# One area for normed tiles and three form pairs, a later load for the third chunk, and one more projection turned by DMA

## The chip, the cores and the metric

The kernel runs on one core of a Trainium2 chip. The metric is the device time of one execution in microseconds (us). The core's engines work in parallel, each through its own list of instructions in order: PE (TensorE, the matrix multiplier, with PEld for its weight loads), DVE (VectorE), ACT (ScalarE), POOL (GpSimd) and SP (SyncE, which here only issues transfers). Transfers are moved by 16 DMA engines; results of PE lie in PSUM until DVE or ACT fetches them.

## The reference

Two layers follow each other on 2048 rows of 576 numbers. Each layer adds a windowed attention (32 heads of 18 numbers, a window of 8 keys at distances 0, 2, ... 14) and a feed-forward block (FFN, 576 to 4608 to 576 with SiLU) to its input; both take the layer-normed input. Weights are the same in both layers.

```python
x = A_x
x = x + _A_ref(_layernorm(x, axis=-1), A_wqkv, A_wo)
x = x + _B_ref(_layernorm(x, axis=-1), B_w1, B_w2)
x = x + _A_ref(_layernorm(x, axis=-1), A_wqkv, A_wo)
x = x + _B_ref(_layernorm(x, axis=-1), B_w1, B_w2)

# in _A_ref: off = jnp.arange(W) * dil, W, dil = 8, 2
logits = jnp.einsum("bhsd,bhswd->bhsw", q, kg) * scale
o = jnp.einsum("bhsw,bhswd->bhsd", softmax(logits), vg)
# _B_ref: silu(x @ w1) @ w2
```

## The kernel before

The 2048 rows are cut into four chunks of 512 rows (`NC = 4`), each of four tiles of 128 rows (`NJ = 4`). Two layers of four chunks make eight stages, s = 0 to 7. A stage is: the products for queries, keys and values (L672), the attention on DVE (L770 to L811), the projection with the output weights `wo` (`project`, L842), and the FFN.

Every product is made of f16 parts: a number is split into a high part (`hi`, on ACT) and the rest (`lo`, on DVE), and the large products of the two are summed. Stages 0 and 1 use a plain FFN (`ffn`: L1181 for the first matrix, L1183 to L1188 for SiLU and the split of its result `h`, L1200 for the second). From stage 2 on (`S2 = 2`) `ffn_pairs` takes the 36 blocks of the hidden layer in 18 pairs q, with seven products P1 to P7 of 256 rows by sums and differences of halves in place of eight (L1084), which DVE adds together (L1091) out of four PSUM tiles (z0, z1, misc0, misc1) that the next products need; then SiLU, the split of h (L1114 on ACT, L1117 on DVE) and L1139 for the second matrix, in six groups of three pairs. The sums and differences of the weights, `wfs`, are made once, by `prepare(q)` on POOL, DVE (L989, L1004) and ACT (L997) during stages 1 and 2, stored, and loaded by `load_wf` (L1014), seven loads for each q, in every stage from 2 on.

What the products take on the other side is made by `forms` (L1021): the four tiles of a chunk are normed, sums and differences are formed, and for each of the seven P a pair of two "yf" tiles is filled by ACT (L1049, L1050) and DVE (L1054, L1055) and turned by two DMA transposes on SP (L1059) into an "xf" tile in the area xb or its neighbours. There are two places for such a pair: one shares its memory with the tiles "yh" (area YH; a normed tile, or one of the attention's output, that is to be turned), the other with "y" and the turned tiles "oT" of the projection (area YO). A place can be filled again once its two transposes have landed. A third place for the pair's hidden sums, "ha", also lies in YO; it is used in stage 2 only. In the profile the names yh and yo stand for everything in these two areas.

`transposed` turns a 128 by 1152 tile in one of two ways: on PE, nine transposes into PSUM (L456) and one copy by ACT (L458), or by one DMA transpose on SP (L460). `project` takes the first for s < 2 and the second from s = 2 on.

The order of the work is not written out. Each operation is given to `Plan` with an engine, a cost, a priority and what it reads and writes; the plan simulates the engines with these costs, takes at each moment the operation of the best priority that has its inputs and its places, and writes the lists of the engines in the order that comes out. Tiles of most names are handed out by turns, and SP has at most eight transfers on the way. So any edit that changes a place, a wait or a cost can change the lists of all engines from there on.

Of the kernel before, what the change touches and what calls it, by code (L numbers as in the profile page):

```python
# [16 lines left out]
P = 128  # L17
# [246 lines left out]
def sliding_attention_silu_ffn(ctx: ExitStack, tc: tile.TileContext, x, wqkv, wo, w1, w2, out):  # L264
# [48 lines left out]
    WQA, W1A, HA = area("wq", 2 * 30 * UC * 2), area("w1", 12 * KB * 2), area("h", 10 * 2 * TB * 2)  # L313
    HSA, YO = area("hs", 3 * TB * 4), area("yo", 2 * 9 * P * 2)

# [22 lines left out]
    tag("mx", 2, [P, NJ, UH], F32, turns=False)  # L338
    part("y", YO, 2, [D], F32, turns=False)
    part("oT", YO, 2, [9, P], F16, turns=False)  # L340
    YH = area("yh", 2 * 9 * P * 2)
    part("yh", YH, 2, [9, P], F16, turns=False)
    parts("yf", [(YH, 0), (YO, 0)], [2, KB], F16)
    tag("wo", 1, [P, 10, D], F16)
# [9 lines left out]
    part("hs", HSA, 3, [TB], F32)  # L354
    parts("ha", [(HSA, 0), (XB, 14 * KB * 2), (YO, 0)], [4, 2 * P], F32)
    parts("hq", [(HSA, 0), (WQA, 20 * 3 * UC), (WQA, 20 * 3 * UC + 32 * P)], [4, 2 * P], F32)
# [109 lines left out]
    gate = []  # L466
    formed = []
    begun = []
    highs = []
# [348 lines left out]
    def project(s, o, xs):  # L818

        pr_ = s - 1.0  # L820
        for j in range(NJ):
            oh, oT, acc = Buf("yh"), Buf("oT"), Buf("acc")

            def hi(j=j, oh=oh):
                f, src = fl(T(oh)), T(o)[:, j, :]
                if s < 2:
                    nc.scalar.activation(f[:, 0:D], src, AF.Copy, scale=SO)
                else:
                    nc.vector.tensor_scalar(f[:, 0:D], src, SO, None, op0=ALU.mult)

            def lo(j=j, oh=oh):
                halves_lo(T(o)[:, j, :], fl(T(oh)), SO)
            src = [(o, j, u) for u in range(NU)] + ["so"]
            op(*(("ACT", 0.7) if s < 2 else ("DVE", 0.45)), hi, src, [(oh, 0)], pr_)
            op("DVE", 0.86, lo, src + [(oh, 0)], [(oh, 1)], pr_)
            transposed(oh, lambda oT=oT: T(oT), oT, j, pr_, s < 2)

            def mm(oT=oT, acc=acc):
                pl = list(passes(lambda k: T(oT)[:, k, :], lambda k: T(WO)[:, k, :]))
                for n, (a, b) in enumerate(pl):  # L840
                    for h in range(2):
                        nc.tensor.matmul(T(acc)[:, h, 0:288], a, b[:, h * 288:(h + 1) * 288],  # L842
                                         start=n == 0, stop=n == len(pl) - 1)
            op("PE", 3.43, mm, [(oT, j)] + [(WO, k) for k in range(10)], [acc], pr_)
            op("DVE", 0.75, lambda j=j, acc=acc: add_to(xs[j], acc, DO), [acc, "so"], [xs[j]], pr_ - 0.3)
# [165 lines left out]

    def load_wf(q, i, prio):
        w = Buf("wf")
        op("SP", 0.38, lambda: nc.sync.dma_start(fl(T(w)), wfs[q][:, i * KB:(i + 1) * KB]), [("wfs", q, i // 4)], [w], prio, nbytes=P * KB * 2)  # L1014
        return w
# [5 lines left out]
    def forms(xs, prio, home="yb", late=[]):  # L1021
# [21 lines left out]
        for n in P_ORDER:  # L1043
            r = Y_ROW[n]
            f, x = Buf("yf"), Buf("xf")
            for a in range(2):
# [5 lines left out]
                def lo(f=f, a=a, r=r):  # L1052
# [5 lines left out]
                done = op("DVE", 0.48, lo, [(ys[a], r), (f, a, 0)], [(f, a, 1)], prio)  # L1058
                op("SP", 1.26, lambda f=f, a=a, x=x: nc.sync.dma_start_transpose(T(x)[:, :, a * P:(a + 1) * P], T(f)[:, a]),  # L1059
                   [(f, a, 0), (f, a, 1)], [(x, a)], prio, nbytes=P * KB * 4)  # L1060
            out[n] = x
# [3 lines left out]
    def ffn_pairs(s, xf, xs):  # L1065
# [3 lines left out]
        for g, n in enumerate(G2):  # L1069
            hb, wbs = [], []  # L1070
            for q in range(q0, q0 + n):
                wf = {k: load_wf(q, W_ROW[k], pd) for k in P_ORDER}
                w2b = [load_w2(2 * q + f, pd, after=begun[-2:-1] if q > q0 + 1 else ()) for f in range(2)]
# [239 lines left out]
```

## Time and profile before

| | us |
|---|---|
| median of 3 runs (2149.39 to 2159.14) | 2149.91 |
| the profiled execution | 2152.02 |
| its span | 2149.9 |
| PE busy | 2110.2 (98%) |
| DVE busy | 1639.7 (76%) |
| ACT busy | 976.4 (45%) |
| POOL busy | 364.5 (17%) |

The span is the profiled part of one execution, 2.1 us less than that execution's own time. "Idle before" is the time for which an engine had nothing running ahead of an instruction, and the name behind the arrow is what ended that. Times within the trace are from the start of the span. PEclk is the clock that PE was granted, as a share of the full one. Lines are those of the kernel before.

### The profile page before, as it was taken

Reading aid. Unit: us, or ns where it says so; the run is one execution under the profiler, and the core shown is the slowest. Engines: PE = TensorE matmul, PEld = TensorE weight load, DVE = VectorE, ACT = ScalarE, POOL = GpSimd, SP = SyncE. Lnnn points to the kernel's source line nnn. Section 1 sums busy time; section 2 is a strip of 40 time slices with the busy share of each in tenths; the row PEclk is TensorE's granted clock in tenths of the full one; section 3 lists DMA queues with packets and bytes.
Section 4 is the critical chain, followed back from the end, with each engine's and each line's share of the span. In section 5 each row is a group of like instructions: output and inputs, shape, how many; then the busy total and the mean of one; then the engine's idle time right before and its main releaser. Section 6 shows DMA issues by size and latency. Waiting matters only on the chain.

```text
span 2149.9 us, 41260 instructions
## 1 busy us (share of the span) xinstructions
PE 2110.2 (98%) x16198; PEld 1578.7 (73%) x16198; DVE 1639.7 (76%) x2585; ACT 976.4 (45%) x1803; POOL 364.5 (17%) x585
## 2 busy tenths in 40 slices
PE   6999999999999999999999999999999999999999
PEld 3556566656666888876788777887788877888887
DVE  8999999999987997648975499755997669853322
ACT  7555787654443553344433343243443434333332
POOL 2224656332432240001100010000000000000000
PEclk9999999999999999999999999999999999999999
DMA  6587778597879987775757756586555965666551
GB/s 181 152 229 250 240 250 266 169 305 256 243 167 258 307 247 215 164 211 171 211 139 191 220 168 179 131 237 190 175 166 142 254 185 158 166 152 197 157 168 62
DMA packets 334233, 426.18 MB, mean 198 GB/s; under 512 B 145608, under 2 KB 262708, under 8 KB 330072
## 3 DMA queue, kind: packets, MB, share of 16 engines
q1 hardware_dynamic: 293720, 293.19, 49.1%
q0 software_dynamic: 38304, 129.28, 18.8%
q8 instruction: 126, 2.06, 0.4%
q10 hardware_dynamic: 2016, 1.11, 0.2%
q14 instruction: 67, 0.55, 0.1%
HBM read 307.32 MB, written 67.68 MB: 174 GB/s over the span
## 4 chain that ended last, share of the span: by engine, by line
PE 71%; DMA 5%; DVE 3%; ACT 1%; issue 0%; SPq 0%; POOL 0%; DVEq 0%; ACTq 0%
PE acc L1139 28%; PE misc L1084 12%; PE z L1084 12%; PE acc L1200 5%; PE z L672 4%; PE acc L842 4%; PE misc L672 3%; PE z L1181 3%; DMA yo<-yh 1%; DMA w<-wfs 1%; DMA xb<-yh 1%; DMA kvs<-kvs 1%; DVE prs L803 0%; DVE prs L770 0%; DVE prs L810 0%
## 5 line engine op out<-in xcount | busy, mean ns | idle before, releaser
L1139 PE MATMUL acc<-w,h 128*128 128x288 f16 x5184 | 669.0, 286 | 0.6 <-DVE x L1148 0.6
L1139 PEld LDWEIGHTS <-h 128*128 128x128 f16 x5184 | 507.7, 98 | 125.7 <-issue 0.8
L1084 PEld LDWEIGHTS <-w 128*128 128x128 f16 x5292 | 517.8, 98 | 73.8 <-issue 5.3
L1084 PE MATMUL misc<-xb,w 128*128 128x256 f16 x2660 | 339.2, 273 | 2.4 <-DVE yo L1091 1.8
L1084 PE MATMUL z<-xb,w 128*128 128x256 f16 x2632 | 332.6, 273 | 3.7 <-DVE hs L1091 2.3
L849 DVE SCALAR_TENSOR_TENSOR x<-acc,d,x 128x576 f32<-128x576 f32 x183 | 148.5, 813 | 140.4 <-PE acc L1139 137.6
L1200 PE MATMUL acc<-w,h 128*128 128x288 f16 x1728 | 217.0, 287 | 3.9 <-DMA w<-wfs 3.7
L672 PEld LDWEIGHTS <-xa 128*128 128x128 f16 x1344 | 131.8, 98 | 111.3 <-issue 2.9
L1200 PEld LDWEIGHTS <-h 128*128 128x128 f16 x1728 | 169.6, 99 | 49.4 <-ACT h L1185 4.0
L770 DVE TENSOR_TENSOR prs<-qt,kvs 128x2304 f32<-128x2304 f32 x64 | 163.5, 2554 | 13.3 <-DMA kvs<-kvs 12.3
L803 DVE TENSOR_TENSOR prs<-kvs,pe 128x1152 f32<-128x1152 f32 x128 | 170.2, 1351 | 0.6
L774 DVE TENSOR_REDUCE lg<-prs 128x128 f32<-128x2304 f32 x64 | 163.1, 2548 | 1.1
L810 DVE TENSOR_TENSOR prs<-prs 128x1152 f32<-128x1152 f32 (+1 forms) x128 | 135.1, 1055 | 2.9
L1181 PE MATMUL z<-xb,w 128*128 128x512 f16 x588 | 130.6, 382 | 3.3 <-ACT w L919 2.6
L1117 DVE SCALAR_TENSOR_TENSOR h<-wq,sh,h 128x1024 f16<-128x1024 f32 x60 | 76.9, 1281 | 71.2 <-ACT h L1114 71.1
L672 PE MATMUL z<-wq,xa 128*128 128x432 f16 x658 | 124.7, 346 | 0.0
L842 PE MATMUL acc<-wo,yo 128*128 128x288 f16 x896 | 114.2, 286 | 3.3 <-DMA yo<-yh 1.5
L1088 ACT ACTIVATE wq<-z 128x256 f32<-128x256 f32 x94 | 35.5, 380 | 172.3 <-PE z L1084 172.3
L1181 PEld LDWEIGHTS <-w 128*128 128x128 f16 x588 | 57.6, 98 | 73.3 <-ACT w L919 3.1
L842 PEld LDWEIGHTS <-yo 128*128 128x128 f16 x896 | 87.4, 98 | 27.8 <-DMA yo<-yh 2.5
L751 POOL DMA_DIRECT2D kvs<-kvs x64 | 33.8, 535 | 415.0 <-ACT qt L741 415.0
L672 PE MATMUL misc<-wq,xa 128*128 128x432 f16 x518 | 100.9, 350 | 0.8 <-ACT qt L741 0.8
(226 smaller groups left out, 2566.6 us busy)
## 6 DMA issues: line engine op xcount, KB each, us to landing
w<-wfs SPq DMA_DIRECT2D x756, 160.0 KB, 3.5
w<-w2s SPq DMA_DIRECT2D x252, 288.0 KB, 4.3
wq<-wqs SPq DMA_DIRECT2D x17, 1080.0 KB, 6.2
kvs<-kd POOLq DMA_DIRECT2D x8, 1584.0 KB, 8.5
w<-w1s SPq DMA_DIRECT2D x36, 320.0 KB, 5.4
wfs<-xa POOLq DMA_DIRECT2D x18, 640.0 KB, 4.6
w2s<-w POOLq DMA_DIRECT2D x36, 288.0 KB, 4.2
w1s<-wq POOLq DMA_DIRECT2D x30, 320.0 KB, 4.1
```

The source lines that it names most:

```text
L672: nc.tensor.matmul(T(m)[:, :3 * UC], a, b, start=n == 0, stop=n == len(pl) - 1)
L770: nc.vector.tensor_tensor(T(pr), T(qt)[:, j:j + 2, None, :].to_broadcast([P, 2, W, UC]), win(T(kv), j, 2), op=ALU.mult)
L774: nc.vector.tensor_reduce(T(lg)[:, j:j + 2].rearrange("p a w h -> p (a w h)"), T(pr).rearrange("p a w (h d) -> p (a w h) d", d=DH), axis=A ...
L803: nc.vector.tensor_tensor(T(pr)[:, a].rearrange("p w (h d) -> p w h d", d=DH), v, T(pe)[:, j + a, :, :, None].to_broadcast([P, W, UH, DH]) ...
L810: nc.vector.tensor_tensor(t[:, :, 0:h, :], t[:, :, 0:h, :], t[:, :, h:2 * h, :], op=ALU.add)
L842: nc.tensor.matmul(T(acc)[:, h, 0:288], a, b[:, h * 288:(h + 1) * 288], start=n == 0, stop=n == len(pl) - 1)
L849: nc.vector.scalar_tensor_tensor(t, T(acc)[:, :, 0:288], d, t, op0=ALU.mult, op1=ALU.add)
L1084: nc.tensor.matmul(t, w[:, u, :], v[:, r, :], start=first and m == 0, stop=m == 6, skip_group_check=True)
L1117: op("DVE", 1.2, lambda hq=hq, h=h, sc=sc: nc.vector.scalar_tensor_tensor(T(h)[:, 1].rearrange("p f t -> p (f t)"), T(hq).rearrange("p r t ...
L1139: nc.tensor.matmul(T(acc)[:, h, 0:288], T(hb[t])[:, a, f, j * P:(j + 1) * P], T(wbs[t][f])[:, w, h * 288:(h + 1) * 288], start=t == 0 and ...
L1181: nc.tensor.matmul(T(z), v, u, start=m == 0, stop=m == len(pl) - 1)
L1200: nc.tensor.matmul(T(acc)[:, h, 0:288], T(hb[q])[:, a, j * P:(j + 1) * P], T(wbs[q][0])[:, w, h * 288:(h + 1) * 288], start=q == 0 and m = ...
```

## The change

Three edits. First, the areas YH and YO become one area, YY, of the same total size (9216 bytes per partition). The tiles yh lie in its first half, y and oT in its second half (from 4608), and three places for form pairs lie at 0, 2560 and 5120; the third place of ha moves to 5120. So three form pairs can be under way at once, and the first two no longer fit the border between yh and oT: the second pair overlaps both. Second, in stage 2 the seven loads of `wfs` for pair q = 1 wait for the last two of the 14 form transposes of that stage. Third, `project` uses the DMA transpose from s = 1 on, where it was from s = 2 on.

```diff
-    HSA, YO = area("hs", 3 * TB * 4), area("yo", 2 * 9 * P * 2)
+    HSA, YY = area("hs", 3 * TB * 4), area("yy", 4 * 9 * P * 2)
+    YO = 2 * 9 * P * 2
...
-    part("y", YO, 2, [D], F32, turns=False)
-    part("oT", YO, 2, [9, P], F16, turns=False)
-    YH = area("yh", 2 * 9 * P * 2)
-    part("yh", YH, 2, [9, P], F16, turns=False)
-    parts("yf", [(YH, 0), (YO, 0)], [2, KB], F16)
+    part("y", YY, 2, [D], F32, at=YO, turns=False)
+    part("oT", YY, 2, [9, P], F16, at=YO, turns=False)
+    part("yh", YY, 2, [9, P], F16, turns=False)
+    part("yf", YY, 3, [2, KB], F16)
...
-    parts("ha", [(HSA, 0), (XB, 14 * KB * 2), (YO, 0)], [4, 2 * P], F32)
+    parts("ha", [(HSA, 0), (XB, 14 * KB * 2), (YY, YO + 512)], [4, 2 * P], F32)
...
-            transposed(oh, lambda oT=oT: T(oT), oT, j, pr_, s < 2)
+            transposed(oh, lambda oT=oT: T(oT), oT, j, pr_, s < 1)
...
-    def load_wf(q, i, prio):
+    def load_wf(q, i, prio, after=()):
...
-        op("SP", 0.38, lambda: nc.sync.dma_start(fl(T(w)), wfs[q][:, i * KB:(i + 1) * KB]), [("wfs", q, i // 4)], [w], prio, nbytes=P * KB * 2)
+        op("SP", 0.38, lambda: nc.sync.dma_start(fl(T(w)), wfs[q][:, i * KB:(i + 1) * KB]), [("wfs", q, i // 4)], [w], prio, nbytes=P * KB * 2, after=after)
...
-                op("SP", 1.26, lambda f=f, a=a, x=x: nc.sync.dma_start_transpose(T(x)[:, :, a * P:(a + 1) * P], T(f)[:, a]),
-                   [(f, a, 0), (f, a, 1)], [(x, a)], prio, nbytes=P * KB * 4)
+                turnings.append(op("SP", 1.26, lambda f=f, a=a, x=x: nc.sync.dma_start_transpose(T(x)[:, :, a * P:(a + 1) * P], T(f)[:, a]),
+                   [(f, a, 0), (f, a, 1)], [(x, a)], prio, nbytes=P * KB * 4))
...
-                wf = {k: load_wf(q, W_ROW[k], pd) for k in P_ORDER}
+                wf = {k: load_wf(q, W_ROW[k], pd, turnings[-2:] if s == S2 and q == 1 else ()) for k in P_ORDER}
```

In the changed kernel the line numbers are one higher from L314 on (L1059 becomes L1060, and so on), and yh and yo are both called yy. The lists are the same up to the projection of stage 1, at some 385 us of the profiled execution of before; they differ on all engines from there to about 950 us, and are nearly the same again behind it, but for the third form pair, which comes earlier. PE loses 36 transposes and their 36 weight loads, ACT the four copies of L458 and three table loads; SP has four DMA transposes more.

In the projection of stage 1 the order of PE is now: four groups of 18 L1201, 14 L1182, 56 L843 (tiles 0 and 1 of the projection), 14 L1182, 18 L1201, 28 L843 (tile 2), 18 L1201, 28 L843 (tile 3). The transposes of tiles 0 and 1 stand on SP ahead of the two loads of w1s2 and w1s3, that of tile 2 behind them, and that of tile 3 behind w1s4 and w1s5; the last two wait for PE, which has to be done with tiles 0 and 1, since oT has two places.

The first place shown is SP towards the end of the first FFN matrix of stage 1, where the forms of stage 2 are turned (about 649 to 671 us of before). w1_70<-wfs0 and wfs1 are the loads for q = 0 and q = 1, xb_67 is where the xf tiles lie. Before:

```order
L1014 DMA w1_70<-wfs0_196 128x640 [waits DMAHW4_49,PE_49]
L1059 DMA_TRANSPOSE xb_67<-yh_91 128x5x128 [waits DMAHW5_49,DVE_49,Activation_49]
L1014 DMA w1_70<-wfs0_196 128x640 [waits DMAHW6_49,PE_49]
L1014 DMA w1_70<-wfs0_196 128x640 [waits DMAHW7_49,PE_49]
L1014 DMA w1_70<-wfs0_196 128x640 [waits DMAHW0_49,PE_49]
L1014 DMA w1_70<-wfs0_196 128x640 [waits DMAHW1_49,PE_49]
L1014 DMA w1_70<-wfs1_197 128x640 [waits DMAHW2_49,DMASW7_49,PE_49]
L1014 DMA w1_70<-wfs1_197 128x640 [waits DMAHW3_49,DMASW6_49,PE_49]
L1014 DMA w1_70<-wfs1_197 128x640 [waits DMAHW4_49,PE_49]
L1059 DMA_TRANSPOSE xb_67<-yo_73 128x5x128 [waits DVE_49,DMAHW5_49,PE_49,Activation_49]
```

The same place in the changed kernel:

```order
L1015 DMA w1_70<-wfs0_195 128x640 [waits DMAHW4_49,PE_49]
L1015 DMA w1_70<-wfs0_195 128x640 [waits DMAHW5_49,PE_49]
L1060 DMA_TRANSPOSE xb_67<-yy_73 128x5x128 [waits DVE_49,DMAHW6_49,PE_49,Activation_49]
L1060 DMA_TRANSPOSE xb_67<-yy_73 128x5x128 [waits DMAHW7_49,DVE_49,Activation_49]
L1060 DMA_TRANSPOSE xb_67<-yy_73 128x5x128 [waits DVE_49,DMAHW0_49,PE_49,Activation_49]
L1060 DMA_TRANSPOSE xb_67<-yy_73 128x5x128 [waits DMAHW1_49,DVE_49,Activation_49]
L1060 DMA_TRANSPOSE xb_67<-yy_73 128x5x128 [waits DVE_49,DMAHW2_49,PE_49,Activation_49]
L1060 DMA_TRANSPOSE xb_67<-yy_73 128x5x128 [waits DMAHW3_49,DVE_49,Activation_49]
L1015 DMA w1_70<-wfs1_196 128x640 [waits DMAHW4_49,DMASW7_49]
L1015 DMA w1_70<-wfs1_196 128x640 [waits DMAHW5_49,DMASW6_49]
```

The last six transposes now stand in one row between the loads for q = 0 and those for q = 1; before, three loads of q = 1 stood ahead of them. Earlier on SP the first six transposes now follow each other at once (before, three, then six loads of w2s between), and the fourth pair's two follow with loads of w2s and w1s between them.

The second place is DVE in the projection of stage 2 (about 564 to 573 us of before), behind the addition of an FFN result to tile x_81. L829 and the two L443 are the split of a tile of the attention's output, which SP then turns, L1188 is the split of h, L1004 is part of `prepare`. Before:

```order
L849 SCALAR_TENSOR_TENSOR x_81<-acc_104,d_269,x_81 128x576 [waits PE_49]
L1004 SCALAR_TENSOR_TENSOR xa<-wq,accw,xa 128x4x256 [waits Activation_49]
L1004 SCALAR_TENSOR_TENSOR xa<-wq,accw,xa 128x4x128 [waits Activation_49]
L1004 SCALAR_TENSOR_TENSOR xa<-wq,accw,xa 128x3x256 [waits Activation_49]
L1004 SCALAR_TENSOR_TENSOR xa<-wq,accw,xa 128x3x128 [waits Activation_49]
L1188 SCALAR_TENSOR_TENSOR h<-hs,sh_266,h 128x512 [waits Activation_49]
L829 TENSOR_SCALAR yh<-o,so 128x576 [waits DMAHW2_49]
```

The same place in the changed kernel:

```order
L850 SCALAR_TENSOR_TENSOR x_81<-acc_103,d_268,x_81 128x576 [waits PE_49]
L830 TENSOR_SCALAR yy<-o,so 128x576 [waits DMAHW6_49]
L443 SCALAR_TENSOR_TENSOR yy<-o,so,yy 128x512 [waits DVE_49]
L443 SCALAR_TENSOR_TENSOR yy<-o,so,yy 128x64
L830 TENSOR_SCALAR yy<-o,so 128x576 [waits DMAHW7_49]
L443 SCALAR_TENSOR_TENSOR yy<-o,so,yy 128x512 [waits DVE_49]
L443 SCALAR_TENSOR_TENSOR yy<-o,so,yy 128x64
```

The splits of tiles 0 and 1 now follow the addition at once; before, four L1004 and one L1188 stood between, and more of them between the two tiles. Ahead of the first instruction of the forms of stage 2 on DVE (L1027) stood the preparations of 8 of the 18 pairs q before, and stand those of 6 now.

The third place is DVE at the start of the pairs of stage 2 (about 697 to 706 us of before). hs and yo are the hidden sums of pairs 0 and 1 (yy and then hs again in the changed kernel), L770 and L774 are attention for the next chunk. Before:

```order
L774 TENSOR_REDUCE lg_86<-prs 128x128 [waits DVE_49]
L1091 TENSOR_TENSOR yo<-z_100,yo 128x256 [waits DMAHW3_49,PE_49,Activation_49]
L770 TENSOR_TENSOR prs<-qt_85,kvs 128x2304 [waits DVE_49]
L1091 TENSOR_TENSOR yo<-misc_103,yo 128x256 [waits DMAHW4_49,Activation_49]
L1091 TENSOR_TENSOR yo<-misc_102,yo 128x256 [waits PE_49]
L1117 SCALAR_TENSOR_TENSOR h<-hs,sh_267,h 128x1024
```

The same place in the changed kernel:

```order
L1092 TENSOR_TENSOR yy<-z_99,yy 128x256 [waits DMAHW0_49,PE_49,Activation_49]
L1092 TENSOR_TENSOR yy<-misc_102,yy 128x256 [waits DMAHW1_49,Activation_49]
L1092 TENSOR_TENSOR yy<-misc_101,yy 128x256 [waits PE_49]
L1118 SCALAR_TENSOR_TENSOR h<-hs,sh_266,h 128x1024
L771 TENSOR_TENSOR prs<-qt_84,kvs 128x2304 [waits DMASW7_49,DMASW6_49,DVE_49]
L775 TENSOR_REDUCE lg_86<-prs 128x128 [waits DVE_49]
L1092 TENSOR_TENSOR hs<-misc_102,hs 128x256 [waits PE_49,Activation_49]
L1092 TENSOR_TENSOR hs<-z_100,hs 128x256 [waits Activation_49]
L1092 TENSOR_TENSOR hs<-z_99,hs 128x256 [waits PE_49]
L1118 SCALAR_TENSOR_TENSOR h<-yy,sh_266,h 128x1024
```

No attention stands between the three additions of pair 1 any more; two of its instructions stand between the first L1118 and the additions of pair 2. Ahead of the first L1117 stood the preparations of 13 of the 18 pairs q before, and stand those of 11 now.

More of the change, by code (lines that the diff above doesn't have):

```diff
@@ L467, in sliding_attention_silu_ffn @@
     formed = []
+    turnings = []
     begun = []
```

## The prediction

> **What bounds the kernel now.** I read the page's busy times first, then what PE waited for, then the windows of the stretch in which the lists differ, then the time order around its longest waits. The page:
>
> ```profile
> span 2149.9 us, 41260 instructions
> ...
> PE 2110.2 (98%) x16198; PEld 1578.7 (73%) x16198; DVE 1639.7 (76%) x2585; ACT 976.4 (45%) x1803; POOL 364.5 (17%) x585
> ...
> PE   6999999999999999999999999999999999999999
> ```
>
> PE bounds: all it does not do is 2149.9 − 2110.2 = 39.7 us, some 20 us of it in the first of the page's 40 slices of 53.7 us, which PE fills to 0.6 and which the change leaves alone. A gain can only be PE work removed, PE waits removed, or a higher clock. PE's waits (us in total, times, longest), those from 385 us on:
>
> ```profile
> PE acc L1200 <- DMA w<-wfs: 3.7, 1, 3.7
> ...
> PE z L1084 <- DVE hs L1091: 2.3, 2, 1.5
> PE misc L1084 <- DVE yo L1091: 1.8, 1, 1.8
> ...
> PE acc L842 <- DMA yo<-yh: 1.5, 2, 0.9
> PE z L1084 <- DMA w<-wfs: 1.3, 1, 1.3
> ...
> PE acc L842 <- DVE x L849: 0.9, 1, 0.9
> ```
>
> Windows (length, busy of PE, PEld, DVE, ACT, POOL, then clock, DMA share, GB/s):
>
> ```profile
> 640.00:660.00 20.00, 19.99 (x98) 9.26 (x97) 11.76 (x22) 13.01 (x24) 6.88 (x10) 1.00 1.13 252
> 660.00:680.00 20.00, 16.26 (x120) 11.94 (x118) 11.43 (x19) 6.43 (x14) 1.50 (x3) 0.91 0.90 180
> 700.00:720.00 20.00, 17.70 (x143) 14.53 (x142) 17.55 (x24) 11.23 (x19) 8.93 (x13) 0.91 1.05 303
> 385.00:570.00 185.00, 184.85 (x1246) 120.24 (x1245) 178.94 (x249) 89.49 (x120) 64.06 (x97) 1.00 0.72 231
> 720.00:860.00 140.00, 140.00 (x1206) 117.70 (x1205) 124.59 (x170) 64.34 (x105) 27.54 (x40) 1.00 0.79 248
> ```
>
> Two windows with a clock of 0.91 lost 0.09 × 20 = 1.8 us each, behind their waits. DVE is nearly full from 385 to 570 (178.94 of 185), so what is moved on DVE there pushes other DVE work later.
>
> **The four projection tiles turned by DMA.**
>
> ```profile
> L456 PE MATMUL acc<-ident,yh 128*128 128x128 f16 x36 | 2.7, 219 | 0.0
> L1200 PE MATMUL acc<-w,h 128*128 128x288 f16 x71 | 9.2, 286 | 0.0
> L458 ACT ACTIVATE yo<-acc x4: 1107/1126/1131, 388.8 to 414.5; 128x1152 f16<-128x1152 f16 x4
> L460 SPq DMA_TRANSPOSE yo<-yh x24: 1280/1703/4095, 570.7 to 1880.9; - x24
> DMA to landing us min/median/max: 3.2/4.0/10.2
> 587.67 3.59 PE L842 MATMUL acc<-wo,yo 128*128 128x288 f16 x28
> 591.10 3.19 PE L1181 MATMUL z<-xb,w 128*128 128x512 f16 x14
> ```
>
> The 36 transposes of 385 to 425 us are 2.7 us of busy time in four groups, each with a pipeline tail of some 0.15 us that the next work covers: 2.0 us of PE. The four ACT copies, 4 × 1.13 us, count nothing: ACT is idle half of that stretch. In their place SP issues four transposes, 1.7 us each, landing 4.0 us later: 5.7 us. The order of PE gives tiles 0 and 1 the 72 L1200 (9.2 us) and 14 L1181 (3.2) to land in; tile 2, which starts when tile 0 has left its place, has 3.6 + 3.2 + 18 L1200 (2.3) = 9.1 us; tile 3 has more. The loads of w1s behind them on SP are moved by 3.4 us and are for the next FFN groups. So −2.0 us; ends: none hidden away, −2.0, and tile 2 late by 4.1 + 10.2 − 9.1 = 5.2 us.
>
> The Trainium skill ("VectorE: DVE Perf Modes", the three transpose paths and the rules for kernel authors) speaks against this edit: it gives 390 ns for a 128x128 transpose on TensorE and 1309 ns by DMA, and advises TensorE where the result may lie in PSUM. By its figures nine blocks would be an estimated 11.8 us by DMA, more than the 9.1 us of cover, and PE would wait; the rows have 4.0 us for all nine, so that I side with the rows.
>
> **The projection of stage 2.** PE waited 1.5 us for two transposes (the L842 row of the waits). They were late since DVE split tile 0 only 3.9 us after the addition ahead of it:
>
> ```profile
> 564.52 0.81 DVE L849 SCALAR_TENSOR_TENSOR x<-acc,d,x 128x576 f32<-128x576 f32 x1
> 569.22 0.52 DVE L829 TENSOR_SCALAR yh<-o,so 128x576 f16<-128x576 f32 x1
> ```
>
> Now the split follows at once, and tile 1's behind it. 3.9 us covers waits of 0.6 and 0.9: −1.5 us. Ends: −1.5 and 0.
>
> **The forms of stage 2.** The wait of 3.74 us, in time order on PE, ACT and SP:
>
> ```profile
> 668.65 0.56 PE L1200 MATMUL acc<-w,h 128*128 128x288 f16 x3 [3.74 <-DMA w<-wfs]
> 660.68 0.44 ACT L1049 ACTIVATE yh<-o 128x288 f16<-128x288 f32 x1 [3.37 <-DMA xb<-yh]
> 666.70 0.44 ACT L1049 ACTIVATE yh<-prs 128x288 f16<-128x288 f32 x1 [5.46 <-DMA xb<-yh]
> 667.87 0.72 ACT L1185 ACTIVATE h<-hs,sh 128x512 f16<-128x512 f32 x1
> 646.97 1.34 SPq L1059 DMA_TRANSPOSE xb<-yh  x1
> 650.03 4.80 SPq L1059 DMA_TRANSPOSE xb<-yh  x1
> 654.93 9.73 SPq L1014 DMA_DIRECT2D w<-wfs  x7
> ```
>
> The load named is not the cause: L1200 resumes when L1185 has made its h, and ACT stood before it behind two fills of a form pair, waiting until transposes issued at 646.97 and 650.03 had landed at 660.7 and 666.7 (13.7 and 16.7 us, at a DMA share of 1.13). With a third place six pairs are filled before most of that FFN group's SiLUs; the forms start up to 11.7 us earlier, since two preparations (5.9 us of DVE each, worked out under the second rival) no longer stand ahead of them on a full DVE; and only the last pair's fill can wait, while the group still has six blocks of 3.2 us to go. Three of q = 1's loads no longer stand ahead of the last transposes. So −3.7 us, and the clock behind it −1.8: −5.5. Ends: −5.5, and 0 if one fill still waits 13 to 17 us ahead of a SiLU. The delayed loads cost nothing: even behind the 666.70 of before they would have 24 us until the pairs' first products at 691.0 (the first L1084 below), and pair 0 comes ahead of them.
>
> **The start of the pairs.**
>
> ```profile
> L1084 PE MATMUL z<-xb,w x378: 272/273/273, 691.0 to 852.6; 128*128 128x256 f16 x189
> 700.81 0.92 PE L1084 MATMUL misc<-xb,w 128*128 128x256 f16 x7 [0.49 <-ACT yo L1088]
> 703.55 1.65 PE L1084 MATMUL misc<-xb,w 128*128 128x256 f16 x7 [1.82 <-DVE yo L1091]
> 700.29 2.55 DVE L770 TENSOR_TENSOR prs<-qt,kvs 128x2304 f32<-128x2304 f32 x1
> 702.75 0.75 DVE L1091 TENSOR_TENSOR yo<-misc,yo 128x256 f32<-128x256 f32 x2
> ```
>
> The 0.49 us is a product that follows another in the same PSUM tile and waits for ACT's copy in between; the 1.82 us is an addition queued behind one attention instruction of 2.55 us. Together 2.3, and the clock 1.8. Now two products follow their like (2 × 0.49 = 1.0), and two attention instructions, 5.1 us, stand ahead of pair 2's additions. PE has 12 L1139 to do meanwhile (1.6 us at the pitch of the like L1200, 9.2 / 71) and six products of at most 0.92, less their tails some 4.6: 6.2 us, against 5.1 + 3 × 0.4 = 6.3 and the second L1118 behind them: I put 1.0 us of waiting there. New waits 2.0, none long enough to lose the clock: −2.3 − 1.8 + 2.0 = −2.1. Ends: −4.1, and, with all 5.1 us bare and the clock lost, +1.
>
> The Trainium skill ("TensorE: Matmul & The Clock Gate", part 1 and the closing rules) has the clock fall only after idle of about 3 us or more. The trace disagrees: it fell behind a wait of 1.82 us. By the rule this clock term would be zero and the sum 1.8 us smaller, 2142.1 us.
>
> **Elsewhere to 950 us** the lists are shuffled on all engines, and new waits of the kind of the 1.5 us on L1091 can arise; from 385 to 570 there were 0.15 us, so the nearest row gives nothing, the largest of this kind 1.5. I take 1.5, since DVE has little slack; ends 0 and 3.3 (the same with a clock loss). Behind 950 us the remaining waits (1.5, 1.3, 0.9) stand in the same order and stay.
>
> **Sum:** −2.0 − 1.5 − 5.5 − 2.1 + 1.5 = −9.6. The execution of 2152.02 becomes 2142.4. It lies 2.1 us over the median, 2149.91, which becomes 2140.3.
>
> **Rivals.**
>
> *The fill still waits.* The last pairs still need earlier transposes to land, and at a DMA share over 1 that took 13.7 and 16.7 us. If the wait of 3.7 us stays or moves, with its clock, the gain is 9.6 − 5.5 = 4.1: 2145.8. For it: SP still issues in order, with loads that wait for PE ahead of the last six transposes. Against: two of three places are new or free earlier.
>
> *DVE becomes the bound behind 690 us* (the slower side). The preparations of two more q fall behind the first L1117. One costs DVE
>
> ```profile
> L989 DVE TENSOR_TENSOR wq<-wq 128x384 f32<-128x384 f32 x72 | 36.9, 553 | 0.8
> L1004 DVE SCALAR_TENSOR_TENSOR xa<-wq,accw,xa 128x1024 f16<-128x1024 f32 x18 | 23.0, 1279 | 0.3 <-ACT xa L997 0.3
> L1004 DVE SCALAR_TENSOR_TENSOR xa<-wq,accw,xa 128x768 f16<-128x768 f32 x18 | 18.2, 1013 | 0.1
> L1004 DVE SCALAR_TENSOR_TENSOR xa<-wq,accw,xa 128x512 f16<-128x512 f32 x18 | 13.4, 747 | 0.0
> L1004 DVE SCALAR_TENSOR_TENSOR xa<-wq,accw,xa 128x384 f16<-128x384 f32 x18 | 11.0, 614 | 0.0
> ```
>
> 4 × 0.553 + 1.279 + 1.013 + 0.747 + 0.614 = 5.9 us, two 11.7. From 700 to 860 DVE was idle for 2.45 + 15.41 = 17.9 us. The point from which it decides is 17.9 us moved into that stretch: with forms of the next chunk also earlier, it may be reached. Then each of the six groups of three pairs has a wait like that of 703, 1.8 us and the clock's 1.8: 6 × 3.6 = 21.6, against the 9.0 of the other terms: +12.6, 2162.5.
>
> *The projection's DMA transposes are late.* Tile 2 by 5.2 us, with the clock 1.8: −9.6 + 7.0 = −2.6, 2147.3. The skill's transpose table above would have it so; the landing row's median bears it out little.
>
> **Chances.** The forecast 0.55 (its own range 2136.8 to 2145.2: the good ends, −2.0 − 1.5 − 5.5 − 4.1 + 0 = −13.1, or the bad ends of the fourth and fifth term, −9.0 + 1.0 + 3.3 = −4.7), the fill 0.18, DVE 0.15, late tiles 0.12. 0.5%, 10.7 us, is about what a measurement of this kernel can tell from no change: the forecast lies just inside it, so half of its chance is faster. Faster 0.28 (all from the forecast); slower 0.17 (DVE 0.15, and 0.02 of late tiles that repeat); same 0.55. The range is 2134 to 2158: below the forecast's own by 2.4 more, the waits of 1.5 and 0.9 us behind 950 us in case they go too; above it lies DVE's 0.15 and little more.
>
> **What would show it.** No L456 after 385 us and no wait of L843 on yy; ACT's L1050 fills waiting less than 3 us between 630 and 670 and no PE wait at L1201; a PEclk of 1.00 in 660 to 720; PE waits on L1092 of 2 us in sum at the first pairs. I am wrong if a wait over 1.5 us stands anywhere between 690 and 860, or if L1050 still waits ahead of a SiLU.

## The result, and the profile after

| | us |
|---|---|
| the changed kernel, median of 6 runs (2161.78 to 2170.08) | 2165.2 |
| the kernel before, median of 6 runs (2149.39 to 2159.47) | 2153.76 |
| ratio, with its 95% interval | 1.0052 [1.0029, 1.0074] |
| profiled execution of the changed kernel, and its span | 2162.65, 2160.7 |

The change made the kernel slower by 0.52%, some 11 us, where a gain of 9.6 us was forecast. The page of the changed kernel:

```profile
span 2160.7 us, 41172 instructions
...
PE 2111.2 (98%) x16162; PEld 1577.3 (73%) x16162; DVE 1639.8 (76%) x2585; ACT 970.8 (45%) x1799; POOL 365.7 (17%) x585
```

PE has 36 matmuls fewer (2.7 us) and is still busy 1.0 us longer, about what the clock losses below come to, 7.0 us against 3.6 before; the rest of the 10.8 us that the span grew is idle time. What PE waited for in the changed kernel (us, times, longest):

```profile
PE acc L843 <- DMA yy<-yy: 8.4, 3, 5.7
PE z L1182 <- ACT hs L1184: 4.6, 2, 4.1
...
PE z L1085 <- DVE hs L1092: 2.5, 2, 1.4
PE misc L1085 <- DMA w<-wfs: 2.3, 3, 1.7
...
PE misc L1085 <- ACT yy L1089: 1.4, 2, 0.9
```

The wait for projection tiles, 1.5 us before, is 8.4: 2.46 of it at 592 us (stage 2), and 5.75 at 813 us in the projection of stage 3, where before there was none. The wait at the forms is still there, 4.13 us at 639 us. Windows of the changed kernel, columns as before:

```profile
580.00:600.00 20.00, 17.54 (x109) 11.14 (x108) 13.76 (x29) 9.24 (x12) 6.91 (x10) 0.91 1.06 220
640.00:660.00 20.00, 17.30 (x74) 7.54 (x74) 16.48 (x26) 13.02 (x23) 6.91 (x10) 0.91 1.02 314
700.00:720.00 20.00, 19.11 (x170) 16.39 (x168) 19.86 (x21) 10.56 (x21) 12.60 (x18) 1.00 1.04 310
810.00:830.00 20.00, 14.19 (x105) 10.81 (x103) 9.56 (x20) 4.45 (x8) 6.33 (x9) 0.83 1.17 245
```

Each of the three long waits has a clock loss, 0.09 × 20 = 1.8 us, 1.8 and 0.17 × 20 = 3.4; before there were two in this stretch, 3.6 in all. The three waits come at a DMA share of 1.02 to 1.17. A share over 1 alone does not make PE wait: in the kernel before it was 1.13 from 640 to 660 us, and PE was busy for 19.99 of these 20 us. In time order, the projection of stage 3 on PE, SP, DVE and POOL of the changed kernel:

```profile
819.16 3.06 PE L843 MATMUL acc<-wo,yy 128*128 128x288 f16 x12 [5.75 <-DMA yy<-yy]
806.17 3.64 SPq L460 DMA_TRANSPOSE yy<-yy  x1
804.61 0.51 DVE L830 TENSOR_SCALAR yy<-o,so 128x576 f16<-128x576 f32 x1
804.63 1.45 POOL L983 DMA_DIRECT2D wq<-in_B_w_dram  x2
809.41 0.58 POOL L1010 DMA_DIRECT2D wfs<-xa  x1 [3.33 <-DVE xa L1005]
811.77 1.44 POOL L979 DMA_DIRECT2D wq<-in_B_w_dram  x2
```

DVE split the tile at 804.6 and SP issued its transpose at 806.17; it landed 13 us later. Around it POOL loads and stores weights of the preparation (L979 and L983 are its loads, L1010 its stores). In the kernel before the last store was issued at 821.2 and the first transpose of that projection at 838.4; in the changed kernel the projection comes 32 us earlier, and the last store, at 857.6, is 36 us later.

### The profile page after: what moved, and what is told of

It is laid out like the page before. It is cut to its first block, busy times and chain, and to the rows that moved or that the text cites. A ratio compares the mean times of both kernels' runs of the same rounds, so it can differ in the third digit from the quotient of the medians.

```text
span 2160.7 us, 41172 instructions
## 1 busy us (share of the span) xinstructions
PE 2111.2 (98%) x16162; PEld 1577.3 (73%) x16162; DVE 1639.8 (76%) x2585; ACT 970.8 (45%) x1799; POOL 365.7 (17%) x585
## 4 chain that ended last, share of the span: by engine, by line
PE 87%; DMA 7%; DVE 2%; issue 2%; ACT 1%; POOL 0%; SPq 0%; ACTq 0%; POOLq 0%; DVEq 0%
PE acc L1140 29%; PE misc L1085 12%; PE z L1085 12%; PE acc L1201 9%; PE z L1182 9%; PE z L673 6%; PE misc L673 5%; PE acc L843 5%; DMA w<-wfs 2%; DMA yy<-yy 1%; DMA h<-in_A_wqkv_dram 1%; DMA w<-w2s 1%; DMA kvs<-kvs 0%; DMA xb<-yy 0%; DVE prs L771 0%
## 5 line engine op out<-in xcount | busy, mean ns | idle before, releaser
L1085 PE MATMUL z<-xb,w 128*128 128x256 f16 x2646 | 337.7, 273 | 4.5 <-DVE hs L1092 2.5
L1085 PE MATMUL misc<-xb,w 128*128 128x256 f16 x2646 | 334.3, 273 | 3.7 <-DMA w<-wfs 2.3
L1201 PE MATMUL acc<-w,h 128*128 128x288 f16 x1728 | 215.3, 286 | 0.0
L1201 PEld LDWEIGHTS <-h 128*128 128x128 f16 x1728 | 169.1, 98 | 44.5
L1118 DVE SCALAR_TENSOR_TENSOR h<-wq,sh,h 128x1024 f16<-128x1024 f32 x60 | 76.9, 1281 | 87.0 <-ACT h L1115 87.0
L1182 PE MATMUL z<-xb,w 128*128 128x512 f16 x588 | 132.0, 385 | 7.8 <-ACT hs L1184 4.1
L843 PE MATMUL acc<-wo,yy 128*128 128x288 f16 x896 | 117.6, 292 | 9.4 <-DMA yy<-yy 8.4
L1182 PEld LDWEIGHTS <-w 128*128 128x128 f16 x588 | 58.0, 99 | 78.7 <-issue 8.4
L843 PEld LDWEIGHTS <-yy 128*128 128x128 f16 x896 | 89.0, 100 | 34.8 <-DMA yy<-yy 9.5
```

Of the source, the lines that this page charges most:

```text
L1085: nc.tensor.matmul(t, w[:, u, :], v[:, r, :], start=first and m == 0, stop=m == 6, skip_group_check=True)
L1118: op("DVE", 1.2, lambda hq=hq, h=h, sc=sc: nc.vector.scalar_tensor_tensor(T(h)[:, 1].rearrange("p f t -> p (f t)"), T(hq).rearrange("p r t ...
L1182: nc.tensor.matmul(T(z), v, u, start=m == 0, stop=m == len(pl) - 1)
L1201: nc.tensor.matmul(T(acc)[:, h, 0:288], T(hb[q])[:, a, j * P:(j + 1) * P], T(wbs[q][0])[:, w, h * 288:(h + 1) * 288], start=q == 0 and m = ...
```

## The experiments

Theory A, formed from this: the third edit lets the attention and with it the projections pass the weight preparation, and their DMA transposes then share the DMA engines with its loads. Its first rival, theory B: the shared area costs, since tiles and form pairs wait for each other.

**One and two edits alone.** The edits are those of the change, none altered.

```diff
-    HSA, YO = area("hs", 3 * TB * 4), area("yo", 2 * 9 * P * 2)
+    HSA, YY = area("hs", 3 * TB * 4), area("yy", 4 * 9 * P * 2)
...
-    parts("yf", [(YH, 0), (YO, 0)], [2, KB], F16)
+    part("yf", YY, 3, [2, KB], F16)
```

```diff
-                wf = {k: load_wf(q, W_ROW[k], pd) for k in P_ORDER}
+                wf = {k: load_wf(q, W_ROW[k], pd, turnings[-2:] if s == S2 and q == 1 else ()) for k in P_ORDER}
```

```diff
-            transposed(oh, lambda oT=oT: T(oT), oT, j, pr_, s < 2)
+            transposed(oh, lambda oT=oT: T(oT), oT, j, pr_, s < 1)
```

e1_area has the first with all that belongs to the area, e2_late the second with the list of the turnings, e3_dma the third; e12_no_dma has the first two and e23_no_area the last two.

> Only the first edit (one area, three form pairs). Theory A (the loss comes from the third edit, whose reshuffle puts the projection of stage 3 among the last weight preparations): the lists keep their order up to 560 us, the wait of 3.7 us at the forms shrinks or goes, no wait over 3 us at the projection of stage 3; time 0 to 6 us under before. Theory B (the shared area itself costs, since pairs, projection tiles and hidden sums now wait for each other): 5 to 11 us over before, with waits on yy at the forms and projections.

> Only the second edit (the loads for pair q = 1 wait for the last form transposes). Both theories: the fills that waited for transposes at 660 and 667 us of before wait less, since three loads leave the queue ahead of the last six; 0 to 4 us under before. If the late loads themselves are what costs, PE waits for w<-wfs at the first products of q = 1 (about 694 us), 1 to 4 us over before.

> Only the third edit (the projection of stage 1 turned by DMA). Theory A: this edit carries most of the loss: 4 to 11 us over before, with a wait of more than 3 us for a DMA transpose at the projection of stage 3, which comes more than 20 us earlier than before. Theory B: PE loses 2.0 us of transposes and nothing else changes: 1 to 4 us under before.

> The first and second edits, without the third. Theory A: the wait at the forms goes, no wait over 3 us at the projection of stage 3: 2 to 8 us under before. Theory B: most of the loss stays: 5 to 11 us over before.

> The second and third edits, without the shared area. Theory A: as the third edit alone, 6 to 12 us over before (the late loads take up to 4 us off its wait at the first pairs). Rival (the loss needs all three): within 4 us of before.

| kernel | ratio to before, 95% interval | PE idle 240 to 950 us | 950 to 2130 us |
|---|---|---|---|
| before | | 8.1 | 4.7 |
| e1_area | 1.0038 [1.0019, 1.0058] | 10.2 | 10.1 |
| e2_late | 1.0001 [0.9986, 1.0016] | 8.6 | 4.3 |
| e3_dma | 1.0047 [1.0032, 1.0062] | 15.7 | 5.0 |
| e12_no_dma | 1.0012 [1.0002, 1.0022] | 4.3 | 7.6 |
| e23_no_area | 1.0041 [1.0023, 1.0059] | 15.0 | 5.4 |
| the change, all three | 1.0052 [1.0029, 1.0074] | 14.4 | 6.8 |

The idle columns are the length of the window less PE's busy time in it, from the profiled execution of each. That is one execution and not always a typical one: that of e12_no_dma lies 4.6 us under the median of its ten (2148.25 against 2152.87), that of e1_area 3.6 us over its median. The ratios are the firmer figure. The third edit carries the loss with or without the others (theory A), though not at the place that I expected. Alone it makes PE wait at the projection of stage 2, the forms and the first pairs:

```profile
PE z L1181 <- ACT hs L1183: 6.3, 2, 5.8
PE z L1084 <- DMA w<-wfs: 5.9, 2, 4.7
PE acc L842 <- DMA yo<-yh: 3.8, 1, 3.8
```

The first edit alone costs too, 0.38% or 8 us, which theory A had not foreseen and which lies in theory B's range. But its longest waits were not those of theory B: they were for late weights, at 657 and 701 us (the second row stands behind 950 us, where its idle time grew most, from 4.7 to 10.1):

```profile
PE z L1084 <- DMA w<-wfs: 5.1, 3, 3.9
PE z L1084 <- DVE hs L1091: 4.0, 2, 2.3
PE z L1181 <- DMA w<-w1s: 3.9, 1, 3.9
```

With the second edit these two go. The wait of 3.74 us at the forms is gone with the first edit alone. With the second alone 1.47 us of it is left, but PE then waits 1.68 and 2.33 us for loads of `wfs` at 693 and 701 us, about where the expectation has the price of the late loads, and e2_late is no faster than before. The fills of form pairs on ACT in e12_no_dma that waited longest for a transpose at that place:

```profile
629.82 0.44 ACT L1050 ACTIVATE yy<-o 128x288 f16<-128x288 f32 x1 [2.25 <-DMA xb<-yy]
...
646.58 0.44 ACT L1050 ACTIVATE yy<-prs 128x288 f16<-128x288 f32 x1 [0.84 <-DMA xb<-yy]
```

So the first two edits together do what the prediction's third term says, and PE idles 3.8 us less up to 950 us; 2.9 us more idle time stand behind it. This one execution is 3.8 us shorter than the profiled one of before (2148.25 against 2152.02), but over all executions the kernel is not under before; where the others lose the rest, no trace shows.

**The loads of the preparation made small, lists unchanged.** The planner is told nothing of this edit, so every list and wait stays as it was; only the POOL loads of `prepare` move less.

```diff
+                rows = 8 if q >= 16 else P
...
-                    nc.gpsimd.dma_start(t[:, h:4:2, k, :], w1[h * KH + k * P:h * KH + (k + 1) * P, 2 * q * P:(2 * q + 2) * P].rearrange(
+                    nc.gpsimd.dma_start(t[0:rows, h:4:2, k, :], w1[h * KH + k * P:h * KH + k * P + rows, 2 * q * P:(2 * q + 2) * P].rearrange(
...
-                    nc.gpsimd.dma_start(t[:, h + 2 * f, 2, :], bass.AP(tensor=v.tensor, offset=v.offset, ap=[[0, 4], *v.ap]))
+                    if rows == P:
+                        nc.gpsimd.dma_start(t[:, h + 2 * f, 2, :], bass.AP(tensor=v.tensor, offset=v.offset, ap=[[0, 4], *v.ap]))
+                    else:
+                        nc.gpsimd.dma_start(t[0:rows, h + 2 * f, 2, :], v[0:rows])
```

This is f1; in the other three kernels the bound is 6 in place of 16. The cut pairs thus combine only 8 of the 128 rows of each weight block that they should.

> The changed kernel with every list left as it is, but the preparation of the last two pairs (q = 16, 17) loads 8 of the 128 rows of each of its pieces (those pairs' weights are then wrong). Theory A (the projection of stage 3 waits since its transposes share the DMA engines with the loads of the late preparations): the wait of 5.75 us at 813 us falls below 1.5 us and the clock loss behind it goes; 5 to 9 us under the changed kernel, 2 to 6 us over before. Rival (the transpose is late because SP or DVE come to it late, or because of the weight loads on SP): the wait stays above 4 us and the time within 2 us of the changed kernel.

> The same for the pairs q = 6 to 17 (8 of 128 rows loaded, wrong weights for these pairs), lists unchanged. Theory A for all three places: the waits at 592 (2.46 us), 639 (4.13) and 813 us (5.75) all fall below 1.5 us and their clock losses go; 10 to 16 us under the changed kernel. Rival (only the projection of stage 3 suffers from these loads, the forms wait for their own transposes and for SP's order): the waits at 592 and 639 stay, and the time is that of the run with the last two pairs cut, within 2 us.

> The same cut of the loads for q = 6 to 17 in the kernel before (wrong weights for these pairs), lists unchanged. Theory A: its waits of 0.63, 0.85 and 3.74 us at the projection and the forms of stage 2 go with the clock loss of 1.8: 4 to 8 us under before. Rival: the 3.74 us stays, within 2 us of before.

> The third edit alone, lists unchanged, with 8 of 128 rows of each piece loaded by the preparation of pairs 6 to 17 (wrong weights for these pairs). Theory A (contention with the preparation's loads is the whole cost): the waits of 3.8 us at 592 us, 5.8 at 651 and 4.7 at 705 fall below 1 us each; 1 to 3 us under the kernel before with the same cut, that is 2 to 5 us under before. Rival (the new order as such): waits of 3 us or more stay, 4 us or more over before.

| kernel | ratio to before | its kernel without the cut |
|---|---|---|
| f1_small_last2 (change, q = 16, 17 cut) | 1.0025 [1.0008, 1.0042] | 1.0052 |
| f2_small_after (change, q = 6 to 17 cut) | 0.9994 [0.9982, 1.0006] | 1.0052 |
| f3_small_before (before, q = 6 to 17 cut) | 0.9988 [0.9976, 1.0000] | 1 |
| k2_small_dma (third edit, q = 6 to 17 cut) | 0.9954 [0.9939, 0.9970] | 1.0047 |

Cutting the loads of the last two pairs alone takes away the wait at the projection of stage 3. The same window as above, in f1_small_last2:

```profile
810.00:830.00 20.00, 20.00 (x168) 16.27 (x167) 14.46 (x27) 6.22 (x9) 1.15 (x3) 1.00 0.70 180
```

The other two waits were smaller in that execution too, 0.72 and 2.36 us in place of 2.46 and 4.13, and without a clock loss, though no load that runs there was cut:

```profile
570.00:600.00 30.00, 29.27 (x185) 17.83 (x184) 27.12 (x43) 15.88 (x21) 7.66 (x11) 1.00 0.93 226
630.00:650.00 20.00, 17.64 (x82) 7.91 (x81) 15.54 (x26) 13.12 (x24) 6.91 (x10) 1.00 1.08 332
```

So one and the same list gives waits that differ by 1.7 us from one execution to the next, and a single wait is weak evidence. The profiled execution of f1 lies 7.5 us under its median (2149.01 against 2156.56). With the loads from q = 6 on cut, both waits are gone, and the times tell f2 from f1, whose intervals do not meet (up to 1.0006, from 1.0008). Windows of f2_small_after:

```profile
570.00:600.00 30.00, 30.00 (x189) 18.36 (x188) 28.02 (x44) 17.29 (x23) 5.73 (x10) 1.00 0.72 186
630.00:650.00 20.00, 20.00 (x94) 9.11 (x93) 15.96 (x25) 11.19 (x20) 5.63 (x10) 1.00 0.83 266
```

and in k2_small_dma PE idles 2.2 us from 240 to 950 us, against 15.7 without the cut. The waits of the third edit's order are thus made by these loads, not by the order as such: with the loads cut that order is 0.46% faster than the kernel before (10 us, where I had expected 2 to 5), and 0.34 points better than that kernel with the same cut. That the loads do it by filling the DMA engines is argued from the shares (1.09 and 1.13 in the change from 570 to 600 and 630 to 650 us, 0.72 and 0.83 in f2); the runs do not tell it from a wait in some queue. In the kernel before the cut removes the 3.74 us at the forms and leaves 3.5 us of idle time up to 950 us; its time falls by 0.12%, 2.6 us, less than the 4 to 8 that I had expected. The profiled spans of f3 and k2, 2140.8 and 2135.4 us, differ by 5.4 us: PE's busy time by 3.0 (2107.4 to 2104.4, with 36 matmuls fewer), its idle time from 240 to 2130 us by 2.0 (3.5 + 3.0 against 2.2 + 2.3); the other 0.4 lies outside of that window. So the gain that the third edit was to bring is there, once nothing collides.

**Attempts to undo the passing.** In g1 the projection of stage 3 waits for the last stored weights, in i1 and i2 the keys of the attention of stage 3 wait for the stored weights behind which they came before, in m1 and m2 the planner is told twice the bytes for the preparation's loads.

```diff
-            src = [(o, j, u) for u in range(NU)] + ["so"]
+            src = [(o, j, u) for u in range(NU)] + ["so"] + ([("wfs", NP - 1, 1)] if s == NC - 1 else [])
```

```diff
-                op("SP" if s == 1 else "POOL", 1.05, fetch, [("qd", c, u), ("qd0", u) if blk == 0 else ("eds", lay, par, u)],
+                op("SP" if s == 1 else "POOL", 1.05, fetch, [("qd", c, u), ("qd0", u) if blk == 0 else ("eds", lay, par, u)] + ([("wfs", (4, 6, 11, 13)[u], 1)] if s == NC - 1 else []),
```

```diff
-        op("POOL", 4.8, load, ["wsc"], [w], prio, nbytes=P * 12 * P * 4, lanes=8)
+        op("POOL", 4.8, load, ["wsc"], [w], prio, nbytes=P * 12 * P * 8, lanes=8)
```

The first is g1, on the change. The second is i1 on the third edit alone and i2 on the change. The third is m1 and m2, on the kernels k1 and h1 that are described below.

> The changed kernel, where the split of the attention's output for the projection of stage 3 also waits for the last stored weights of the preparation, as it came behind them before; all lists are as in the changed kernel up to there. Theory A: the wait of 5.75 us at the projection of stage 3 goes with its clock loss, 5 to 9 us under the changed kernel. Rival (the wait is owed to the queue of weight loads in the pairs and would come up wherever the projection stands): a wait of 3 us or more at that projection stays, within 3 us of the changed kernel.

> The third edit alone, with the attention of stage 3 held back: its four loads of keys wait for the stored weights of pairs 4, 6, 11 and 13, behind which they came before. Theory A (the third edit costs only since it lets attention pass the preparation, which then runs into the transposes of the projection and the forms of stage 2): most of the 10 us that the third edit costs alone come back, within 4 us of before, and the waits at the forms of stage 2 (5.8 us) and at the first pairs (4.7) fall below 2. Rival (the four transposes on SP are themselves what costs, or any new order does): the time stays 6 to 12 us over before.

> The changed kernel with the attention of stage 3 held back in the same way. Theory A: the waits at 592, 639 and 813 us of the changed kernel fall below 1.5 us each; 8 to 14 us under the changed kernel, from 3 us under to 3 us over before. Rival: within 4 us of the changed kernel.

> All three edits, two form pairs behind stage 2, and the planner told twice the bytes for the preparation's loads. If the planner only lacks their price: the waits for DMA transposes at 590 to 810 us (11 us with two pairs behind stage 2) fall below 4 us in all, 4 to 12 us under that kernel, at or under before. Rival (another order, other collisions): waits of 8 us or more stay somewhere between 560 and 860 us, within 5 us of that kernel.

> The first and second edits, two form pairs behind stage 2, and the planner told twice the bytes for the preparation's loads. If the planner only lacks their price: 0 to 4 us under the same without it. Rival: 2 to 12 us over it, with new waits for transposes or loads.

| kernel | ratio to before |
|---|---|
| g1_proj3_late | 1.0081 [1.0058, 1.0105] |
| i1_dma_keep | 1.0058 [1.0038, 1.0077] |
| i2_all_keep | 1.0043 [1.0022, 1.0064] |
| m1_dear_loads | 1.0047 [1.0032, 1.0063] |
| m2_dear_loads | 0.9990 [0.9974, 1.0005] |

None helped. i2, m1 and m2 came out as their rivals had it; g1 and i1 came out worse than theirs, g1 6.2 us over the change (rival: within 3) and i1 12.5 us over before (rival: 6 to 12). Waits went at one place and came at another. In g1 there is no wait at the projection of stage 3, but PE waits for the form transposes of that stage, which now come late (at 920 us); in i1 for the same ones (at 911 us); in i2 two fills hold up the SiLU at 633 us for longer than ever; in m1 the projection of stage 3 waits for DVE; m2 waits 1.5 to 2.0 us for a weight load and for transposes at 648, 836 and 920 us, where h1 did not. From g1, i1, i2 and m1, in this order, one line of PE's waits each:

```profile
PE misc L1085 <- DMA xb<-yy: 5.0, 1, 5.0
```

```profile
PE misc L1084 <- DMA xb<-yh: 4.7, 1, 4.7
```

```profile
PE z L1182 <- ACT hs L1184: 15.1, 2, 14.6
```

```profile
PE acc L844 <- DVE x L851: 5.7, 2, 5.4
```

The last two are waits for transposes too, at second hand. ACT's fills in i2, and the split on DVE ahead of the addition that m1's PE waited for:

```profile
633.02 0.44 ACT L1050 ACTIVATE yy<-o 128x288 f16<-128x288 f32 x1 [9.71 <-DMA xb<-yy]
642.69 0.44 ACT L1050 ACTIVATE yy<-prs 128x288 f16<-128x288 f32 x1 [9.10 <-DMA xb<-yy]
```

```profile
794.01 0.52 DVE L831 TENSOR_SCALAR yy<-o,so 128x576 f16<-128x576 f32 x1 [9.81 <-DMA yy<-yy]
```

Putting the preparation nearly back where it was thus does not bring the time back. "The preparation is passed" is too narrow a cause. What the cut runs show is that its loads make the transposes late at all three places of the change; that the five orders here only moved the meeting is argued, since no loads were cut in them. The profiled execution of i1 lies 11.6 us under its median (2155.13 against 2166.69), so it understates what the others waited.

**Two form pairs behind stage 2.** Theory C: the third pair costs in stages 4 to 7. The time order of DVE in the changed kernel at 1698 us shows how it can: the additions that PE waits for stand behind the norm statistics of a tile whose load came late. PE waits 1.41 us there; why the load was late is not shown.

```profile
1697.99 0.82 DVE L507 BATCH_NORM_STATS2 st<-x 128x6 f32<-128x288 f32 x2 [3.07 <-DMA x<-xd]
...
1699.59 0.41 DVE L1092 TENSOR_TENSOR hs<-z,hs 128x256 f32<-128x256 f32 x1
```

```diff
     part("yf", YY, 3, [2, KB], F16)
+    part("yg", YY, 2, [2, KB], F16)
...
-    def forms(xs, prio, home="yb", late=[]):
+    def forms(xs, prio, home="yb", late=[], pairs="yf"):
...
-            f, x = Buf("yf"), Buf("xf")
+            f, x = Buf(pairs), Buf("xf")
```

> The first and second edits, but three form pairs in stage 2 only, two in the stages behind it. Theory C (the third pair costs in stages 4 to 7, where the form transposes now stand ahead of the weight loads of the pairs and the first pairs wait for loads and additions): PE's waits behind 950 us fall from 7.1 us to between 3 and 5; 2 to 4 us under the first and second edits with three pairs throughout, that is 0 to 2 us under before. Rival (those waits come from run to run): behind 950 us 6 us or more stay, and the time is that of the two edits within 1 us.

> The first and second edits with two form pairs behind stage 2, again. If its 0.26% hold: 0.9960 to 0.9985 of before; the waits at the forms of stage 2 and the clock losses behind 240 us are gone.

> All three edits, but two form pairs in stages 3 to 7. Theory C (a third pair behind stage 2 is a cost of its own of 3 to 8 us): 3 to 8 us under the changed kernel, 3 to 8 over before. Rival (it costs only together with the first two edits' order): within 2 us of the changed kernel.

The call of forms gives `"yf" if s == S2 else "yg"` as the last argument. h1 has the first two edits of the change beside this, k1 all three.

| kernel | ratio to before | PE idle 240 to 950 us | 950 to 2130 us |
|---|---|---|---|
| h1_two_later | 0.9974 [0.9958, 0.9990] | 4.7 | 3.9 |
| h1_again | 0.9980 [0.9964, 0.9996] | 2.5 | 3.3 |
| k1_all_two_later | 1.0044 [1.0027, 1.0062] | 13.9 | 5.6 |

Of the kernels here that leave nothing out, h1 alone is faster than before, by 0.20 to 0.26%. It is 7 to 8 us under e12_no_dma, where I had expected 2 to 4. All seven profiled kernels with three pairs throughout have 6.8 to 10.7 us of PE idle time behind 950 us, the twelve others, before among them, 2.3 to 6.0. Part of this is chance: the change, f1 and f2 have the same lists, and 6.8, 9.5 and 8.5 us. In time it is seen between e12_no_dma (1.0012) and h1, whose intervals do not meet; between the change and k1 (1.0052, 1.0044) the intervals overlap, and the 1.7 us lie where the rival had them (within 2), so there it isn't settled. In k1 most of the idle time is one wait, at the projection of stage 3:

```profile
PE acc L844 <- DMA yy<-yy: 11.1, 3, 9.5
```

## Why the prediction was wrong

Term by term, in the profiled executions. *The four tiles by DMA* (−2.0): right in itself. From 385 to 570 PE did not wait:

```profile
385.00:570.00 185.00, 185.00 (x1221) 119.39 (x1220) 177.14 (x247) 79.67 (x110) 56.77 (x86) 1.00 0.74 227
386.94 3.06 SPq L460 DMA_TRANSPOSE yy<-yy  x2
```

The rival of late tiles (0.12) did not happen there; tiles were late at the two projections behind it, for another reason. *The projection of stage 2* (−1.5): wrong, the wait grew by 1.0 to 2.46, with a clock loss of 1.8. The step that failed is "they were late since DVE split tile 0 only 3.9 us after the addition". DVE did split tile 0 at once, at 562.2, 7.0 us earlier than before, and the wait for it (0.63) is gone. But the larger wait of before, 0.85, was for the third tile, and that one's split hardly moved. Before:

```profile
582.48 0.52 DVE L829 TENSOR_SCALAR yh<-o,so 128x576 f16<-128x576 f32 x1
584.84 2.33 SPq L460 DMA_TRANSPOSE yo<-yh  x1
595.14 3.60 PE L842 MATMUL acc<-wo,yo 128*128 128x288 f16 x28 [0.85 <-DMA yo<-yh]
```

In the changed kernel:

```profile
582.22 0.51 DVE L830 TENSOR_SCALAR yy<-o,so 128x576 f16<-128x576 f32 x1
583.78 5.73 SPq L460 DMA_TRANSPOSE yy<-yy  x2
594.34 5.89 PE L843 MATMUL acc<-wo,yy 128*128 128x288 f16 x33 [2.46 <-DMA yy<-yy]
```

PE came to it 2.4 us earlier than before, at 591.9, and the transpose landed only 0.8 us earlier, more than 10 us after its issue as before. With the preparation's loads cut (f2) the wait was gone.

*The forms of stage 2* (−5.5): 4.13 us and 1.8 us of clock stayed, as in the rival "the fill still waits", which gave 2145.8 for it. With the first two edits alone the term was right (no wait at that place in e12_no_dma, nor in h1). With the third edit the first six transposes stood in a row from 619 on and took 11.4 us to issue. The fills behind them, which need their places, waited 7.13, 2.11, 3.72 and 1.63 us one after another, and the SiLU that PE waited for (L1184) stood behind these:

```profile
619.15 11.43 SPq L1060 DMA_TRANSPOSE xb<-yy  x6
630.25 0.44 ACT L1050 ACTIVATE yy<-prs 128x288 f16<-128x288 f32 x1 [7.13 <-DMA xb<-yy]
...
637.67 0.44 ACT L1050 ACTIVATE yy<-o 128x288 f16<-128x288 f32 x1 [3.72 <-DMA xb<-yy]
...
641.98 0.67 ACT L1184 ACTIVATE hs<-z,d 128x512 f32<-128x512 f32 x1
```

*The start of the pairs* (−2.1): right, a little small. Two waits behind ACT's copies, 0.47 and 0.89 us, in place of 2.3, and the clock stayed at 1.00: −1.0 − 1.8 = −2.8. The 1.0 us of waiting put there for pair 2's additions did not come.

*Elsewhere to 950 us* (+1.5, ends 0 and 3.3): the step that failed. I took the nearest row for it from the stretch 385 to 570, and the largest wait of one kind; what came was a wait of another kind, 5.75 us and 3.4 us of clock, +9.2, at a projection that I had not looked at, though the lists had it ahead of the last preparations. *Behind 950 us* (stay): 4.7 became 6.8, +2.1, where I had held the order for nearly the same. With the first term as forecast, all six come to −2.0 + 2.8 + 0.4 − 2.8 + 9.2 + 2.1 = +9.7, of the 10.6 us between the two profiled executions.

The rival "DVE becomes the bound" (0.15, nearly all of the chance that I gave a slower kernel) did not happen, and that its 2162.5 is close to the measured time is an accident: from 720 to 860 DVE was busy for 121.1 of 140 us, less than the 124.6 of before:

```profile
720.00:860.00 140.00, 133.97 (x1129) 110.93 (x1127) 121.10 (x187) 66.67 (x107) 40.39 (x58) 0.98 0.83 234
```

I had looked for the price of the deferred preparation on DVE, where I could add it up, and not on the DMA engines, though the forms' own rows, landings of 13.7 and 16.7 us at a share of 1.13, showed it. So the direction was wrong: the third edit, priced at −2.0, cost 0.4 to 0.5% with the waits that came with it.

## What to carry to other kernels

Where a planner makes the order, an edit that saves engine time can cost more through what it moves: look in the new lists for every transfer that something waits for, and see which bulk transfers it now shares the DMA engines with. An experiment that cuts the data of the suspected transfers but leaves all lists as they are tells what these transfers cost from what the order itself costs; holding work back by new waits doesn't, since it makes a third order. Judge such runs by the times of many executions: the same list had waits that differed by 1.7 us from one profile to another. Try the parts of a joint edit apart: here two of the three, cut back to the stage they were meant for, made the kernel 0.2 to 0.26% faster.

## What the runs showed of the hardware

A DMA transpose of a projection tile, which lands in 4.0 us in the median, took 13 us beside the strided weight loads of POOL, and on SP up to 6.4 us to issue (1.7 in the median). And the length of a wait does not alone decide over the clock. It fell behind 1.82 us in the kernel before, but not behind 3.83 us in e3_dma, nor behind 2.82 us at 648 us in i1_dma_keep, nor behind the 2.36 us of f1_small_last2 (its row of 630 to 650 us above):

```profile
570.00:600.00 30.00, 26.17 (x160) 15.36 (x159) 24.05 (x37) 17.29 (x23) 7.08 (x10) 1.00 1.11 239
```

```profile
640.00:660.00 20.00, 17.15 (x80) 7.49 (x79) 8.29 (x18) 9.61 (x20) 1.90 (x3) 1.00 1.09 246
```

The Trainium skill ("TensorE: Matmul & The Clock Gate", part 1) says that the window in which activity is counted runs free of the kernel; that would let a short wait hit and a longer one miss, and these rows agree with it as far as they go, though 1.82 us is well under the idle time that the page names. No run here settles what decides.
